# Low parts of four weight tiles and of two batches' probabilities, made by an adding DMA onto the negative of the high parts

## The chip, the core and the metric

The kernel runs on one core of a Trainium2 chip. The metric is device time in microseconds for one execution, from launch to end. The core has a matrix engine (TensorE; PE in the profile, PEld for its weight loads), a vector engine (VectorE, DVE), an activation engine (ScalarE, ACT), a general engine (GpSimd, POOL) and SyncE (SP), which here only issues DMAs. Each engine runs its own instructions in order; they wait for each other through semaphores.

## The reference

Attention through a packed set of 32 queries per head, followed by a feed-forward network with an ELU between its two matrices. For 8 batches, 8 heads, 576 positions and head size 64:

```python
p_packed = sm_attn(p, k, v)          # 32 packed queries read the keys and values
out = sm_attn(q, p_packed, p_packed) # every position reads the 32 packed ones
x = out.transpose(0, 2, 1, 3).reshape(B * S, H * D)      # 4608 x 512
h = x @ w_in                                             # 512 -> 2048
g = np.where(h > 0.0, h, np.exp(np.minimum(h, 0.0)) - 1.0)
return (g @ w_out).astype(np.float32)                    # 2048 -> 512
```

The two weight matrices arrive as 64-bit floating-point words; the core turns them into 32-bit ones itself, from their mantissa, exponent and sign.

## The kernel before

**The products.** The feed-forward input isn't formed. For each batch and each quarter `c` of the 2048 hidden columns, `mstep` multiplies the packed attention result by `w_in` (L705) into a tile `m`; the hidden values are then the probabilities `a` of the second attention times `m` (`mm`, L815 and L822). The hidden columns are taken in 16 tiles of 128, `f` = 0 to 15, and each batch in two halves of its 576 positions. One step of the main loop is one (batch, half, `f`): product `mm`, then ACT's Relu (L829) and Exp (L835), then DVE's maximum (L838), which gives the ELU value `g`, then the second product with `w_out` (`out_mm`, L932 to L941), which is issued 3.5 steps later in the plan.

**High and low parts.** Most products are made in a faster 32-bit format of the matrix engine (`F32R`). An operand is split into a high part, a copy into that format, and a low part, word minus high part; three products of parts stand for one product. For `w_out` the parts are `wo(f, 0)` and `wo(f, 1)`, made by `high` (a copy, on ACT) and `low` (a subtraction, on DVE, L331). For the probabilities they are `a_hi` and `a_lo`, made in `attention` by `hi` (a copy, L252) and `lo` (a subtraction, L658), one pair of instructions per half of a batch. The start works without these parts: batches 0 and 1 use whole words for `c` = 0 (`H_PLAIN`, L815) and for the first four tiles of `w_out` (`F_PLAIN`, L932), whose words lie in `w_words`. Their parts are made all the same, since batches 0 and 1 need `a_hi` and `a_lo` from `f` = 4 on, and batches 2 to 7 need all of `w_out` in parts.

**The weights.** `weights(f, first, prio)` converts one tile of `w_in` (`first`) or of `w_out`: `load` by SP into `raw` (three buffers for both matrices), `exponent` (L280), `sign` (L292), `power` (L287), `mantissa` into `mi` (two buffers, L295), `whole` (L301), the last reader of `raw`, `signed` (L308) and `product` (L318). The product of a `w_in` tile goes to `w_in_sb`, that of the first four `w_out` tiles to `w_words`, that of the others back into `mi`, from which `high` and `low` then read. Tiles `f` of 8 and more lie in `wo_b`, whose memory is that of the first batches' temporary tiles; `home_op` stands for the moment at which these are free.

**The order.** Nothing is put in order by hand. Every operation is entered by `op(prio, engines, function, deps, take, use)` with a due number and an estimated time for each engine that may do it. `schedule()` plays this out greedily: at each moment the ready operation of the lowest due number starts on its engine if the engine and all its buffers are free. Due numbers are steps of the main loop: `first_use` of what is made, less a lead such as `LI`, `LO` or `LM`, or plus `T_WS` (high and low parts of the first four `w_out` tiles) or `T_AS` (those of the first two batches' probabilities). A released buffer is one whose users' estimated ends are past. What the plan gives to each engine is then that engine's order on the chip.

**Output.** Finished sums go through `part` to HBM, first parts by SP, later parts by an adding DMA issued on POOL (L964).

Of the kernel before, what the change touches and what calls it, by code (L numbers as in the profile page):

```python
# [9 lines left out]
F32 = mybir.dt.float32  # L10
# [5 lines left out]
ALU = mybir.AluOpType  # L16
# [4 lines left out]
def packed_attention_elu_ffn(  # L21
# [19 lines left out]
    nc = tc.nc  # L41
# [22 lines left out]
    WC = NPAIR * P  # L64
# [13 lines left out]
    T_ATT, T_ATT1 = [12, 14.0, 15.0, 16.0, 17.5, 17.5], [-12, -11, -11, -10, -10, -9]  # L78
    LI, LO, LM, LOOK = 4.5, 3.0, 2.5, 3.5
    TM = [24.5, 24.5, 28.0, 28.0]  # L80
    T_S2, STAY, SWITCH = 0, 4, 0.12

    F_PLAIN, H_PLAIN = 4, [0, 1]
    T_WS, T_AS = 20, 6

# [55 lines left out]
    def op(prio, on, fn, deps=(), take=(), use=(), after=(), mode=None):  # L145
        o = Op()
        o.prio, o.on, o.fn, o.deps = prio, on, fn, [d for d in deps if d is not None]
        o.after = [d for d in after if d is not None]
        o.take, o.end, o.n, o.mode = list(take), None, len(ops), mode
        for b in list(take) + list(use):  # L150
            b.users.append(o)
        ops.append(o)
        return o

    def schedule():
# [81 lines left out]
        raw=3, ex=2, sg=1, mi=2, p=2, ppT=3, pp=1, k0=1, q0=1,  # L237
# [7 lines left out]
    def wo(f, part):  # L245
        return wo_a[:, f, part, :] if f < NFA else pools["wo_b"][:, f - NFA, part, :]
# [4 lines left out]
    def copy(e, out, in_):  # L251
# [3 lines left out]
    w_ready, w_split, conv_ops = {}, {}, []  # L255

    w_words = [
        Buf(R["m_lo"], lambda: mpool.tile([P, 2, E], F32, tag="m_lo", name="w_words"))
        for _ in range(F_PLAIN // 2)
    ]  # L260

    def weights(f, first, prio):

        raw = ring_tile("raw", stg, [P, WC, 2], U32, "raw", bufs=3)
        ex_b = ring_tile("ex", stg, [P, WC], U16, "ex")
        sg_b = ring_tile("sg", stg, [P, WC], BF16, "sg", bufs=1)
        mi_b = ring_tile("mi", stg, [P, WC], U32, "mi")

        def words():
            r = raw.t  # L270
            top = r.rearrange("p n t -> p (n t)").bitcast(U16).rearrange("p (n t) -> p n t", t=4)
            return r[:, :, 0], r[:, :, 1], top[:, :, 3]

        def load(e):
            nc.sync.dma_start(  # L275
                out=raw.t.rearrange("p n t -> p (n t)"), in_=(w_in if first else w_out)[f]
            )

        def exponent(e):
            nc.vector.tensor_scalar(  # L280
                out=ex_b.t, in0=words()[2], scalar1=4, scalar2=0x7FF,
                op0=ALU.logical_shift_right, op1=ALU.bitwise_and,
            )

        def power(e):

            nc.scalar.activation(  # L287
                out=ex_b.t.bitcast(BF16), in_=ex_b.t, func=AF.Exp, scale=LN2, bias=ebias
            )

        def sign(e):
            nc.scalar.activation(out=sg_b.t, in_=words()[1].bitcast(F32), func=AF.Sign)  # L292

        def mantissa(e):
            nc.vector.tensor_scalar(  # L295
                out=mi_b.t, in0=words()[1], scalar1=0xFFFFF, scalar2=0x100000,
                op0=ALU.bitwise_and, op1=ALU.bitwise_or,
            )

        def whole(e):  # L300
            nc.vector.scalar_tensor_tensor(  # L301
                out=mi_b.t.bitcast(F32), in0=words()[0], scalar=2.0 ** -32, in1=mi_b.t,
                op0=ALU.mult, op1=ALU.add,
            )

        def signed(e):
            pw = ex_b.t.bitcast(BF16)
            nc.vector.tensor_tensor(out=pw, in0=pw, in1=sg_b.t, op=ALU.mult)  # L308

        def product(e):  # L310
            ms, pw = mi_b.t.bitcast(F32), ex_b.t.bitcast(BF16)
            out = ms
            if plain:
                out = word()
            if first:
                out = w_in_sb[:, :, f * P:(f + 1) * P]
                ms, pw = (x.rearrange("p (c f) -> p c f", c=NPAIR) for x in (ms, pw))
            nc.vector.scalar_tensor_tensor(  # L318
                out=out, in0=ms, scalar=2.0 ** -20, in1=pw, op0=ALU.mult, op1=ALU.mult
            )  # L320

        plain = not first and f < F_PLAIN

        def word():
            return w_words[f // 2].t[:, f % 2, :] if plain else mi_b.t.bitcast(F32)

        def high(e):
            copy(e, wo(f, 0), word())

        def low(e):  # L330
            nc.vector.tensor_tensor(  # L331
                out=wo(f, 1), in0=word(), in1=wo(f, 0).bitcast(F32), op=ALU.subtract
            )

        ld = op(-60 + f if first and f < 4 else -44 + f / 9 if f < 2 else prio - 8, {"DMA": 1.45}, load, take=[raw])
        x = op(prio, {"DVE": 0.42}, exponent, [ld], take=[ex_b], use=[raw])
        s = op(prio, {"ACT": 0.66}, sign, [ld], take=[sg_b], use=[raw])
        p = op(prio, {"ACT": 0.72}, power, [x], use=[ex_b])
        m = op(prio, {"DVE": 0.42}, mantissa, [ld], take=[mi_b], use=[raw])
        w = op(prio, {"DVE": 0.69}, whole, [m], use=[raw, mi_b])  # L340
        g = op(prio, {"DVE": 0.42}, signed, [p, s], use=[ex_b, sg_b])
        words_b = w_words[f // 2:f // 2 + 1] if plain else []
        take = words_b if f % 2 == 0 else []
        last = op(
            prio, {"DVE": 0.69}, product, [w, g], take=take,
            use=[mi_b, ex_b] + [b for b in words_b if b not in take],
            after=[w_ready[False, f - 1]] if words_b and f % 2 else [],
        )
        if plain:

            h = op(T_WS + f, {"ACT": 0.61}, high, [last], use=words_b)
            w_split[f] = op(T_WS + f, {"DVE": 0.69}, low, [h], use=words_b)
        elif not first:
            home = [home_op] if f >= NFA else []
            h = op(prio, {"ACT": 0.61}, high, [last] + home, use=[mi_b])
            last = op(prio, {"DVE": 0.69}, low, [h], use=[mi_b])
        w_ready[first, f] = last
        conv_ops.append(last)

# [9 lines left out]
    def attention(b, ts):  # L369

        st, prev_b = Batch(), sts.get(b - 1)
# [18 lines left out]
        whole = b in H_PLAIN  # L390
# [65 lines left out]
        for name, fn, bufs, t in (  # L456
            ("k", load_k, k_b, ts[0] - 6), ("v", load_v, v_b, ts[0] - 5), ("q", load_q, q_b, ts[0] - 3),
        ):
            lds[name] = []
            for n, x in enumerate(bufs):  # L460
                prev_ld = op(
                    t, {"DMA": 3.3 / len(bufs)}, lambda e, fn=fn, n=n: fn(e, n),
                    take=[x] + ([p_b] if (name, n) == ("k", 0) else []), after=[prev_ld],
                )
                lds[name].append(prev_ld)
# [40 lines left out]
        def srec1(e):  # L506
# [6 lines left out]
        o1 = op(ts[0], {"PE": 1.0}, s1, ld_k, take=ps1 + e1s, use=[p_b] + k_b,  # L513
                after=[prev_b.tmp_last if b > 1 else None], mode=1)
        o4s, o = [], None
        for g in range(G):
            o = op(ts[0], {"DVE": 0.76}, lambda e, g=g: smax1(e, g), [o1], use=[ps1[g]], after=[o])
            o = op(ts[0], {"DVE": 0.16}, lambda e, g=g: neg(e, g), [o])
# [4 lines left out]
        for g in range(G):  # L523
# [19 lines left out]
            t = ts[1]  # L543
# [20 lines left out]
        o = op(ts[2], {"PE": 0.85}, pv, ld_v + tr_done, take=[ps, pp_b], use=v_b + e1T, mode=2)  # L564
        done = []
        for g in range(G):
            def norm(e, g=g, ps=ps):
# [10 lines left out]
                use=[ps, pp_b],  # L578
# [11 lines left out]
        o = op(ts[3], {"PE": 0.06}, tr2, done, take=[pt2, st.ppT], use=[pp_b])  # L590
# [3 lines left out]
        for half in range(2):  # L594
            ps = banks(2)
            t1, t2 = temp(), st.af if whole else temp()
# [47 lines left out]
            cs = slice(half * HS, (half + 1) * HS)  # L644

            def done(t2=t2, cs=cs):
                if whole:
                    return st.af.t[:, :G, cs]
                return flat(t2).rearrange("p (g s) -> p g s", g=G)
# [4 lines left out]
            def hi(e, cs=cs, done=done):  # L654
                copy(e, st.a.t[0][:, :, cs], done())

            def lo(e, cs=cs, done=done):
                nc.vector.tensor_tensor(  # L658
                    out=st.a.t[1][:, :, cs], in0=done(), in1=st.a.t[0][:, :, cs].bitcast(F32),
                    op=ALU.subtract,  # L660
                )

            t = ts[4 + half]
            o = op(t, {"PE": 0.52}, s2, [lds["q"][half % len(q_b)], st.ppT_op],
                   take=[ps, t1], use=[q_b[half % len(q_b)], st.ppT], mode=1)
            f0 = op(t, {"DVE": 0.44}, lambda e, fold=fold: fold(e, 0), [o] + prev, use=[ps, t1])
            f1 = op(t, {"DVE": 0.44}, lambda e, fold=fold: fold(e, 1), [f0], use=[ps, t1])
            o = op(t, {"DVE": 0.75}, smax, [f1], use=[t1])
            o = op(t, {"DVE": 0.76}, ssub, [o], use=[t1])
# [11 lines left out]
                t, {"ACT": 0.67, "DVE": 0.4}, hi, [o] + st.a_done[-1:],  # L681
                take=[st.a] if half == 0 else [], use=[t2] + ([st.a] if half else []),
            )
            st.a_done.append(op(t, {"DVE": 0.75}, lo, [h], use=[t2, st.a]))
        st.tmp_last = prev[0]
        st.m, st.m_done = {}, {}
        return st
# [327 lines left out]
```

## Time and profile before

| what | value |
|---|---|
| median of three runs | 725.33 us (725.0 to 726.03) |
| the profiled execution's own time | 724.5 us |
| its span, first to last instruction | 722.3 us |
| granted clock of TensorE, mean | 0.998 |
| PE busy | 699.6 us, 97% of the span |
| PEld busy | 557.1 us, 77% |
| DVE busy | 504.4 us, 70% |
| ACT busy | 387.4 us, 54% |
| POOL busy | 19.4 us, 3% |

The span is the time between the first and the last instruction that the profiler recorded; 2.2 us of the execution's time lie around it. Busy time is the union of an engine's instructions. The shares are means over the whole span: the first hundred microseconds, in which the weights are converted and the first batches run, look different from the rest, so windows of the span are read beside the page. A row of a group shows the line, the engine, the operation, what is written and what is read, and how often; then times. A row of the chain of waits shows the start, the length and what ran.

### The profile page before, as it was taken

Reading aid. Unit: us, or ns where it says so; the run is one execution under the profiler, and the core shown is the slowest. Engines: PE = TensorE matmul, PEld = TensorE weight load, DVE = VectorE, ACT = ScalarE, POOL = GpSimd, SP = SyncE. Lnnn points to the kernel's source line nnn. Section 1 sums busy time; section 2 is a strip of 40 time slices with the busy share of each in tenths; the row PEclk is TensorE's granted clock in tenths of the full one; section 3 lists DMA queues with packets and bytes.
Section 4 is the critical chain, followed back from the end, with each engine's and each line's share of the span. In section 5 each row is a group of like instructions: output and inputs, shape, how many; then the busy total and the mean of one; then the engine's idle time right before and its main releaser. Section 6 shows DMA issues by size and latency. Waiting matters only on the chain.

```text
span 722.3 us, 13401 instructions
## 1 busy us (share of the span) xinstructions
PE 699.6 (97%) x5076; PEld 557.1 (77%) x5076; DVE 504.4 (70%) x1256; ACT 387.4 (54%) x900; POOL 19.4 (3%) x27
## 2 busy tenths in 40 slices
PE   2799999999999999999999999999999999999997
PEld 1454588887778877888878887888888877888886
DVE  6999998886875587545875569555686559654453
ACT  5777888885654455434454445434454345444332
POOL 0000002110111000000000000000000000000000
PEclk9999999999999999999999999999999999999999
DMA  9846546634543430003300250001400040000010
GB/s 348 296 150 204 186 147 142 132 66 108 165 59 44 123 108 1 30 1 128 117 2 29 67 165 1 2 29 66 160 21 1 30 132 30 1 30 1 0 45 30
DMA packets 29360, 61.42 MB, mean 85 GB/s; under 512 B 2544, under 2 KB 11760, under 8 KB 29040
## 3 DMA queue, kind: packets, MB, share of 16 engines
q1 hardware_dynamic: 26272, 55.06, 22.6%
q0 software_dynamic: 3024, 5.51, 5.6%
q8 instruction: 40, 0.66, 0.4%
q14 instruction: 24, 0.20, 0.1%
HBM read 45.61 MB, written 14.94 MB: 84 GB/s over the span
## 4 chain that ended last, share of the span: by engine, by line
PE 96%; DVE 1%; DMA 1%; ACT 1%; issue 0%; SPq 0%; ACTq 0%
PE psum L822 27%; PE psum L938 18%; PE psum L939 17%; PE psum L941 17%; PE psum L932 4%; PE psum L705 4%; PE psum L815 2%; PE psum L557 2%; PE psum L531 1%; PE psum L476 1%; PE psum L602 1%; DMA k<-in_kT 1%; DVE mx L486 0%; ACT tmp L500 0%; SPq L275 0%
## 5 line engine op out<-in xcount | busy, mean ns | idle before, releaser
L829 ACT ACTIVATE e<-psum 128x256 f32<-128x256 f32 (+1 forms) x256 | 105.4, 412 | 236.2 <-PE psum L822 214.4
L838 DVE SCALAR_TENSOR_TENSOR e<-e,psum 128x256 f32<-128x256 f32 (+1 forms) x240 | 103.6, 432 | 106.8 <-ACT e L835 106.1
L822 PE MATMUL psum<-a_hi,m_hi 128*128 128x256 f32 (+1 forms) x480 | 146.5, 305 | 0.0
L822 PE MATMUL psum<-a_lo,m_hi 128*128 128x256 f32 (+1 forms) x480 | 142.0, 296 | 0.0
L822 PE MATMUL psum<-a_hi,m_lo 128*128 128x256 f32 (+1 forms) x480 | 141.9, 296 | 0.0
L861 DVE TENSOR_TENSOR g_lo<-e,g_hi 128x256 fp32r<-128x256 f32 (+1 forms) x240 | 105.3, 439 | 22.0 <-ACT g_hi L252 7.1
L835 ACT ACTIVATE e<-e 128x256 f32<-128x256 f32 (+1 forms) x256 | 114.0, 445 | 6.1
L938 PE MATMUL psum<-wo_b,g_hi 128*128 128x512 f32 x288 | 114.8, 398 | 0.0
L939 PE MATMUL psum<-wo_b,g_hi 128*128 128x512 f32 x288 | 113.6, 394 | 0.0
L822 PEld LDWEIGHTS psum<-a_hi,m_hi 128*128 128x128 f32 x480 | 90.5, 189 | 24.2 <-issue 9.6
L938 PE MATMUL psum<-wo_a,g_hi 128*128 128x512 f32 x252 | 99.4, 394 | 0.0
L939 PE MATMUL psum<-wo_a,g_hi 128*128 128x512 f32 x252 | 99.3, 394 | 0.0
L822 PEld LDWEIGHTS psum<-a_lo,m_hi 128*128 128x128 f32 x480 | 90.7, 189 | 8.7 <-issue 1.0
L822 PEld LDWEIGHTS psum<-a_hi,m_lo 128*128 128x128 f32 x480 | 90.6, 189 | 0.0
L941 PE MATMUL psum<-wo_b,g_lo 128*128 128x512 f32 x288 | 86.6, 391 | 0.0
L941 PE MATMUL psum<-wo_a,g_lo 128*128 128x512 f32 x252 | 76.1, 392 | 0.0
L938 PEld LDWEIGHTS psum<-wo_b,g_hi 128*128 128x128 f32 x288 | 54.2, 188 | 12.1 <-issue 3.6
L941 PEld LDWEIGHTS psum<-wo_b,g_lo 128*128 128x128 f32 x288 | 54.1, 188 | 12.1
L252 DVE CAST g_hi<-e 128x256 fp32r<-128x256 f32 (+1 forms) x180 | 54.0, 300 | 12.5 <-PE psum L939 3.7
L939 PEld LDWEIGHTS psum<-wo_b,g_hi 128*128 128x128 f32 x288 | 54.3, 189 | 7.6
L941 PEld LDWEIGHTS psum<-wo_a,g_lo 128*128 128x128 f32 x252 | 47.3, 188 | 10.5
L938 PEld LDWEIGHTS psum<-wo_a,g_hi 128*128 128x128 f32 x252 | 47.5, 188 | 9.4 <-ACT g_hi L252 2.5
(88 smaller groups left out, 761.3 us busy)
## 6 DMA issues: line engine op xcount, KB each, us to landing
out<-part SPq DMA_DIRECT2D x36, 256.0 KB, 2.2
raw<-in_w_in SPq DMA_DIRECT2D x16, 512.0 KB, 3.7
kvq<-in_v SPq DMA_DIRECT2D x16, 512.0 KB, 5.1
raw<-in_w_out SPq DMA_DIRECT2D x16, 512.0 KB, 3.5
kvq<-in_kT SPq DMA_DIRECT2D x14, 576.0 KB, 4.5
kvq<-in_qT SPq DMA_DIRECT2D x14, 576.0 KB, 4.6
out<-part POOLq DMA_DIRECT2D x21, 256.0 KB, 4.4
k<-in_kT SPq DMA_DIRECT2D x1, 1152.0 KB, 7.4
```

Source lines behind the costliest of these rows:

```text
L252: (nc.scalar.copy if e == "ACT" else nc.vector.tensor_copy)(out=out, in_=in_)
L557: nc.tensor.matmul(ps.t[cols_of(pair), g, :D], lhsT=e1T[g].t[:n, c, cols_of(pair)], rhs=values(c, h)[:n], start=(c == 0), stop=(c == NKC - 1),
L705: nc.tensor.matmul(ps.t[cols_of(pair), g, :w], lhsT=st.ppT.t[rows_of(g), pair, :], rhs=w_in_sb[rows_of(g), pair, c * FC + part * w:c * FC ...
L822: nc.tensor.matmul(ps_b.t[:, :n_tok], lhsT=m_b[x].t[:, g, o:o + P], rhs=st.a.t[y][:, g, cols], start=(n == 0), stop=(n == 3 * G - 1),)
L829: nc.scalar.activation(out=e_b.t[:, :n_tok], in_=ps_b.t[:, :n_tok], func=AF.Relu, scale=-1.0)
L835: nc.scalar.activation(out=x, in_=x, func=AF.Exp, scale=-1.0)
L838: nc.vector.scalar_tensor_tensor(out=out, in0=e_b.t[:, cs], scalar=-1.0, in1=ps_b.t[:, cs], op0=ALU.add, op1=ALU.max)
L861: nc.vector.tensor_tensor(out=g_b.t[1][:, cs], in0=x, in1=g_b.t[0][:, cs].bitcast(F32), op=ALU.subtract)
L932: nc.tensor.matmul(a.t, lhsT=g_b.t[0][:, t].bitcast(F32), rhs=w_words[f // 2].t[:, f % 2, :], start=first, stop=final,)
L938: nc.tensor.matmul(a.t, lhsT=g_b.t[0][:, t], rhs=wo(f, 0), start=first, stop=False)
L939: nc.tensor.matmul(a.t, lhsT=g_b.t[0][:, t], rhs=wo(f, 1), start=False, stop=False)
L941: nc.tensor.matmul(a.t, lhsT=g_b.t[1][:, t], rhs=wo(f, 0), start=False, stop=final)
```

## The change

Two kinds of low parts are no longer made by DVE's subtraction. ACT writes the negative of the word, rounded to the same format, to the place of the low part; a DMA issued on POOL then adds the word itself onto it. That is done for the first four `w_out` tiles (`BY_DMA`) and for the probabilities of batches 0 and 1 (`A_DMA` with `whole`). The due numbers of these parts become smaller (`T_WS` from 20 to 16, `T_AS` from 6 to 2). The word of a later `w_out` tile goes into the first half of `raw` instead of `mi`, and `high` and `low` read it there. The due numbers of the first loads are taken from a list, `FIRST`.

```diff
+    FIRST = "i0 i1 i2 i3 k v o0 o1 q".split()
+    BY_DMA, A_DMA = (0, 1, 2, 3), True
...
-    T_WS, T_AS = 20, 6
+    T_WS, T_AS = 16, 2
...
-            out = ms
-            if plain:
-                out = word()
+            out = word()
...
         def word():
-            return w_words[f // 2].t[:, f % 2, :] if plain else mi_b.t.bitcast(F32)
+            return w_words[f // 2].t[:, f % 2, :] if plain else raw.t[:, :WC // 2].rearrange(
+                "p n t -> p (n t)"
+            ).bitcast(F32)
...
+        def minus(e):
+            nc.scalar.mul(wo(f, 1), word(), -1.0)
+
         def low(e):
-            nc.vector.tensor_tensor(
-                out=wo(f, 1), in0=word(), in1=wo(f, 0).bitcast(F32), op=ALU.subtract
-            )
-
-        ld = op(-60 + f if first and f < 4 else -44 + f / 9 if f < 2 else prio - 8, {"DMA": 1.45}, load, take=[raw])
+            if e == "DVE":
+                nc.vector.tensor_tensor(
+                    out=wo(f, 1), in0=word(), in1=wo(f, 0).bitcast(F32), op=ALU.subtract
+                )
+            else:
+                nc.gpsimd.dma_start(out=wo(f, 1).bitcast(F32), in_=word(), accum_op=ALU.add)
+
+        name = ("i" if first else "o") + str(f)
+        t = FIRST.index(name) - 60 if name in FIRST else prio - 8
+        ld = op(t, {"DMA": 1.45}, load, take=[raw])
...
             prio, {"DVE": 0.69}, product, [w, g], take=take,
-            use=[mi_b, ex_b] + [b for b in words_b if b not in take],
+            use=[mi_b, ex_b] + [b for b in words_b if b not in take] + [raw] * (not (first or plain)),
...
             h = op(T_WS + f, {"ACT": 0.61}, high, [last], use=words_b)
-            w_split[f] = op(T_WS + f, {"DVE": 0.69}, low, [h], use=words_b)
+            if f in BY_DMA:
+                h = op(T_WS + f, {"ACT": 0.61}, minus, [h], use=words_b)
+            w_split[f] = op(T_WS + f, {"POOL": 1.0} if f in BY_DMA else {"DVE": 0.69}, low, [h], use=words_b)
         elif not first:
             home = [home_op] if f >= NFA else []
-            h = op(prio, {"ACT": 0.61}, high, [last] + home, use=[mi_b])
-            last = op(prio, {"DVE": 0.69}, low, [h], use=[mi_b])
+            h = op(prio, {"ACT": 0.61}, high, [last] + home, use=[raw])
...
+            last = op(prio, {"POOL": 1.0} if f in BY_DMA else {"DVE": 0.69}, low, [h], use=[raw])
...
+            if b == 0:
+                t = FIRST.index(name) - 60
...
+            def minus(e, cs=cs, done=done):
+                nc.scalar.mul(st.a.t[1][:, :, cs], done(), -1.0)
+
+            def add(e, cs=cs, done=done):
+                nc.gpsimd.dma_start(
+                    out=st.a.t[1][:, :, cs].bitcast(F32), in_=done(), accum_op=ALU.add
+                )
...
-            st.a_done.append(op(t, {"DVE": 0.75}, lo, [h], use=[t2, st.a]))
+            if whole and A_DMA:
+                h = op(t, {"ACT": 0.67}, minus, [h], use=[t2, st.a])
+                h = op(t, {"POOL": 1.0}, add, [h], use=[t2, st.a])
+            else:
+                h = op(t, {"DVE": 0.75}, lo, [h], use=[t2, st.a])
+            st.a_done.append(h)
```

More of the change, by code (lines that the diff above doesn't have):

```diff
@@ L351, in weights @@
             h = op(T_WS + f, {"ACT": 0.61}, high, [last], use=words_b)
-            w_split[f] = op(T_WS + f, {"DVE": 0.69}, low, [h], use=words_b)
+            if f in BY_DMA:
+                h = op(T_WS + f, {"ACT": 0.61}, minus, [h], use=words_b)
+            w_split[f] = op(T_WS + f, {"POOL": 1.0} if f in BY_DMA else {"DVE": 0.69}, low, [h], use=words_b)
         elif not first:
             home = [home_op] if f >= NFA else []
-            h = op(prio, {"ACT": 0.61}, high, [last] + home, use=[mi_b])
-            last = op(prio, {"DVE": 0.69}, low, [h], use=[mi_b])
+            h = op(prio, {"ACT": 0.61}, high, [last] + home, use=[raw])
+            if f in BY_DMA:
+                h = op(prio, {"ACT": 0.61}, minus, [h], use=[raw])
+            last = op(prio, {"POOL": 1.0} if f in BY_DMA else {"DVE": 0.69}, low, [h], use=[raw])
         w_ready[first, f] = last
```

## The prediction

> **What bounds the kernel now.** I read the page's 40 slices first, then the waits of PE, the chain of waits in order of time, and the windows. The waits of PE, longest first (what waited, for what: us in total, times, longest us):
>
> ```profile
> PE psum L476 <- DMA k<-in_kT: 10.1, 1, 10.1
> PE psum L531 <- ACT tmp L500: 5.9, 3, 2.8
> PE psum L476 <- ACT m_hi L252: 1.1, 1, 1.1
> ...
> PE psum L815 <- DVE g_hi L838: 0.2, 1, 0.2
> ```
>
> All but the last of these lie before the first L815 matmul, at 31.6 us. After that PE waits 0.2 us in all. The page warns that a busy PE need not be a PE at its peak, so the chain of waits has to be asked whether matmuls follow each other at one pace (start us, us, what):
>
> ```profile
> 68.14 0.86 PE psum L815 x4
> 69.00 2.58 PE psum L932 x6
> 71.58 0.86 PE psum L815 x4
> ```
>
> Every piece begins where the one before it ends: four L815 matmuls of 256 columns at 0.215 us each, six L932 of 512 columns at 0.43 us each, and so on. There is no idle time hidden in the busy time here. DVE, which the change relieves, is the fullest of the other engines in these stretches (PE, PEld, DVE, ACT, POOL busy us; PE clock; DMA share; GB/s):
>
> ```profile
> 20.00:30.00 10.00, 5.53 (x114) 2.41 (x103) 9.20 (x21) 6.86 (x15) 0.00 (x0) 1.00 0.96 347
> 30.00:40.00 10.00, 9.35 (x109) 6.76 (x108) 9.00 (x22) 8.05 (x21) 0.00 (x0) 0.83 0.64 203
> 60.00:70.00 10.00, 9.85 (x46) 5.41 (x45) 9.89 (x23) 9.48 (x22) 0.00 (x0) 1.00 0.59 189
> 100.00:120.00 20.00, 20.00 (x120) 16.87 (x119) 17.01 (x43) 16.31 (x41) 1.92 (x2) 1.00 0.56 158
> ```
>
> So there are two stages. Before 31.6 us a chain through ACT and DVE sets the time, with PE idle about half. Afterwards PE sets it, and DVE, though 9.9 of 10 us busy at 60 to 70 us, delivers just in time: nearly nobody waits for it. A microsecond taken from DVE after 31.6 us is worth at most the 0.2 us that PE waits; a microsecond taken before it is worth something only on the chain.
>
> **The change part by part.** These are the instructions removed, and the nearest relatives of those added (ns min/median/max, first and last start):
>
> ```profile
> L331 DVE TENSOR_TENSOR wo_a<-w_words,wo_a x4: 674/684/685, 26.0 to 80.1; 128x512 fp32r<-128x512 f32 x4
> L658 DVE TENSOR_TENSOR a_lo<-k,a_hi x2: 694/723/752, 38.3 to 41.5; 128x576 fp32r<-128x576 f32 x2
> L658 DVE TENSOR_TENSOR a_lo<-q,a_hi x2: 747/751/755, 61.8 to 68.2; 128x576 fp32r<-128x576 f32 x2
> L252 ACT CAST wo_a<-w_words x4: 620/633/639, 21.2 to 39.1; 128x512 fp32r<-128x512 f32 x4
> L252 ACT CAST a_hi<-k x2: 657/666/674, 31.1 to 40.8; 128x576 fp32r<-128x576 f32 x2
> 109.94 1.92 POOL L964 DMA_DIRECT2D out<-part  x2 [108.64 <-ACT part L252]
> out<-part POOLq DMA_DIRECT2D x21, 256.0 KB, 4.4
> ```
>
> DVE loses 4 x 0.684 + 2 x 0.723 + 2 x 0.751 = 5.7 us. ACT gains as many scaled copies: 4 x 0.633 + 4 x 0.666 = 5.2 us, with the price of the cast of the same tile. POOL gains eight issues of about 0.96 us (1.92 us for two stores), and it stands idle until 108.6 us, so nothing is queued behind them at first. Seven to eight microseconds of work move, but only the part that touches a bound counts.
>
> *Start, DVE.* One removed subtraction falls before 31.6 us. The rows of batch 0's softmax around it (start us, us, engine, line, operation):
>
> ```profile
> 25.73 0.69 ACT L626 ACTIVATE tmp<-tmp 128x576 f32<-128x576 f32 x1 [0.56 <-DVE tmp L620]
> 25.96 0.67 DVE L331 TENSOR_TENSOR wo_a<-w_words,wo_a 128x512 fp32r<-128x512 f32 x1
> 26.56 0.73 DVE L630 TENSOR_REDUCE sm<-tmp 128x18 f32<-128x576 f32 x1
> 27.23 0.74 DVE L486 TENSOR_REDUCE mx<-psum 128x1 f32<-128x576 f32 x1
> 30.27 0.77 DVE L652 STREAM_TRANSPOSE k<-tmp 128x576 f32<-128x576 f32 x1
> 31.64 2.37 PEld L815 LDWEIGHTS psum<-k,m_hi 128*128 128x128 f32 x7
> ```
>
> The subtraction runs while the exponential (to 26.42 us) holds the chain anyway; the sum L630 comes 0.14 us later. Taking it away gives 0.14 us at least, at most its own 0.67 us if DVE's following fill also moves forward. I take -0.1, since the row right behind it says so. The next of the subtractions on weights stands far behind:
>
> ```profile
> 62.88 0.68 DVE L331 TENSOR_TENSOR wo_a<-w_words,wo_a 128x512 fp32r<-128x512 f32 x1
> ```
>
> So the other seven removed operations start after 31.6 us and are worth between 0 and the 0.2 us that PE waits there; I take 0. DVE's saved time will be filled by weight conversion that has later due times.
>
> *Start, ACT.* A negative copy follows each high part. ACT's idle places there:
>
> ```profile
> 22.38 0.62 ACT L252 CAST wo_a<-w_words 128x512 fp32r<-128x512 f32 x1 [0.54 <-DVE w_words L318]
> 27.71 0.65 ACT L292 ACTIVATE sg<-raw 128x512 bf16<-128x512 f32 x1 [1.30 <-DMA raw<-in_w_out]
> ```
>
> The first copy of 0.63 us fits into a hole of 0.54 and pushes the next cast by 0.1; the second goes into the hole of 0.56 before L626 or the one of 1.30 us. Cost: 0 to 0.6 us; I take +0.1.
>
> *After the start, ACT.* Six more copies fall on an engine that is up to 9.48 of 10 us busy, and each is not interrupted once begun. Where ACT is fullest, the chain already leaves PE:
>
> ```profile
> 62.77 0.24 ACT wo_a L252
> ...
> 63.68 0.50 DVE g_hi L838
> 64.22 1.34 PE psum L815 x4
> ```
>
> An ELU chain (Relu, Exp, DVE maximum) that meets a copy just begun is up to 0.67 us late; two products in flight and the next batch's matmuls cover it nearly everywhere. Bounds: 0 (all hidden) and 6 x 0.65 = 3.9 us; I take +0.2, the size of the one wait of this kind that the rows show.
>
> *The adds.* Their nearest row is the store by adding DMA, 4.4 us to landing. Their results are late only beyond this (ns and first and last start):
>
> ```profile
> L822 PE MATMUL psum<-a_lo,m_hi x480: 278/294/311, 81.8 to 712.1; 128*128 128x256 f32 x80, 128*128 128x320 f32 x80
> L932 PE MATMUL psum<-w_words,g_hi x72: 590/592/697, 37.3 to 88.5; 128*128 128x512 f32 x72
> ```
>
> The first reader of a low probability starts at 81.8 us, while the last of the subtractions replaced is at 68.2; the four weight tiles' low parts aren't read before batch 2, as batches 0 and 1 multiply by the whole words, until 88.5 us. Over 12 us of slack stand against 0.96 + 4.4 = 5.4 us for issue and landing: 0, and a loss only from more than twice that landing time on. The Trainium skill, "SBUF — State Buffer", section "SBUF: two separate sides", speaks against adds issued here: GpSimd can't write their descriptors while a DVE instruction in a two-port mode holds the shared port. No row of before isolates this; the 0.96 us per issue while DVE is 85% busy bears out no long lock. In traffic, one add of 256 KB at the 347 GB/s of 20 to 30 us takes 0.75 us; two beside the first loads delay those by 0 to 1.5 us. They bring batch 1's keys and values, off batch 0's chain: 0.
>
> *The raw buffer.* From the fifth w_out tile on, the word is kept in raw instead of mi, so raw (three buffers, shared with w_in) stays taken until the low part is made. Loads wait for just that release now:
>
> ```profile
> SPq L275 <- DVE mi L301: 80.6, 22, 8.2
> raw<-in_w_in SPq DMA_DIRECT2D x16, 512.0 KB, 3.7
> 102.99 6.38 SPq L275 DMA_DIRECT2D raw<-in_w_in  x2
> 118.91 0.68 DVE L331 TENSOR_TENSOR wo_b<-mi,wo_b 128x512 fp32r<-128x512 f32 x1
> 120.18 0.42 DVE L280 TENSOR_SCALAR ex<-raw 128x512 uint16<-128x512 uint16 x1
> 131.93 0.69 DVE L318 SCALAR_TENSOR_TENSOR w_in_sb<-mi,ex 128x512 f32<-128x512 f32 x1
> 134.24 0.66 PE L705 MATMUL psum<-w_in_sb,ppT 64*32 64x256 f32 x16
> ```
>
> The tightest place: the second of those loads goes out at about 109.0, after L301 of the eleventh w_out tile. With the new release it goes out after that tile's L331, at 119.6, and lands 3.7 us later, at 123.3; its first reader stands at 120.2, so 3.1 us late. Its conversion now takes until 132.6 with pauses of some microseconds in between, and PE needs it at 134.2, 1.6 us of slack. Cost 0 if the pauses shrink, 3.1 - 1.6 = 1.5 us if they don't. In return mi is free earlier, and DVE comes to this stage with up to 5.7 us less behind it: I take 0. A load that waits at the head of SP's queue also holds back the keys, queries and plain stores behind it; these are planned with the same releases, so it is the same term.
>
> The due times of the high and low parts (20 to 16, 6 to 2) move idle-time work; the new list of first loads gives the old order (four of w_in, k, v, two of w_out, q), and is worth 0.
>
> **Sum** against the profiled execution: 724.5 us, 722.3 of span and 2.2 around it. -0.1 + 0.1 + 0.2 + 0 = +0.2, so 724.7. The median of the runs shown, 725.33, is 0.8 above that execution; the forecast on that scale is 725.5.
>
> **Rivals.**
> *Faster: the start shortens.* The chain to 31.6 us carries DVE work not of its own, L486 at 27.23 for one; if the new plan drops one such block, 0.7 us go. One stretch of the start is also clocked down (same columns as the windows above):
>
> ```profile
> 30.20:33.60 3.40, 2.87 (x10) 2.48 (x11) 3.37 (x10) 3.06 (x8) 0.00 (x0) 0.50 0.59 215
> ```
>
> From 31.6 to 33.6 PE runs the bound work at half speed, so 1.0 us is lost there; a plan that keeps PE busier before it would win that, and 0.7 + 1.0 = 1.7 gives 723.6. Against it: the matmuls before it hang on the same waits as now. The Trainium skill, "TensorE: Matmul & The Clock Gate", Part 1, says that an idle window of about 3.4 us halves the clock and that the windows run free of the kernel. The row agrees: 3.4 us at 0.50, behind a stretch in which PE was busy 5.5 of 10 us. By that rule a small shift of the window could also cost as much again, which would give 726.5.
>
> *Slower: the raw buffer starves conversion.* Price 1.5 us at the place above, and once more for the last tiles of w_in, which pass the same three buffers: 725.5 + 3.0 = 728.5. It decides when low parts of w_out wait more than 1.6 us longer than PE's next weights allow. For it: all 22 of the waits above. Against it: mi freed earlier, and DVE time.
>
> *Slower: ACT takes DVE's place.* If three of the six copies land on an ELU chain, 3 x 0.65 = 2.0 us: 727.5. For it, ACT's 9.48 of 10; against it, PE's contiguous pieces.
>
> *Late adds.* From the end of the last replaced subtraction, 68.9, to the first reader, 81.8, there are 12.9 us; issue and landing take 5.4. An add that took 16 us would cost the 3.1 us beyond: 728.6.
>
> *The change doesn't do what it says*: DVE's time is refilled by other work in the same stretch, and PE never learns of it: 725.3.
>
> **Chances.** Forecast (723.9 to 726.8) 0.56; refilled, 0.05; shorter start 0.19; raw buffer 0.10; ACT 0.08; late adds 0.02. A measurement of this kernel can tell about 0.2%, 1.45 us, from no change. So faster 0.19, same 0.61, slower 0.20. The range reaches from 723.2 (just beyond the short start) to 728.0, leaving the tails of the slow cases outside.
>
> **What would show it.** In the changed profile the first L815 should still start within 0.7 us of 31.6, and PE's waits behind it should stay under 1 us. L331 should have 12 rows and L658 12, ACT about 5 us more between 20 and 75 us. Loads of raw should wait for L331 in place of L301. The forecast is wrong if PE waits for L705's weights near 105 to 165 us, or for g_hi between 34 and 80 us, or if the first L815 starts below 30 us.

## The result, and the profile after

The changed kernel takes 729.78 us (median of 4 runs, 728.37 to 730.66) against 725.16 us of the kernel before (four runs, the three of the table above among them): a ratio of 1.0059, 95% interval 1.0044 to 1.0074. It is slower by 0.6%, where no change was forecast, with 728.0 us as the upper end of the range. The profiled execution took 730.66 us, 6.2 us more than the one before; the difference of the medians is 4.6 us. Of the 6.6 us by which its span is longer (728.9 against 722.3), 2.8 us are idle time of PE (25.5 against 22.7) and 3.8 us busy time (703.4 against 699.6, with 5076 matmuls both times). The granted clock differs from run to run, 0.992 to 0.994 in the four runs of the change and 0.992 to 1.000 in 26 of the kernel before, so this split holds for one execution.

The waits of PE in the changed kernel (what waited, for what: us in total, times, longest us; L845 is what L815 was, L574 was L557, L600 was L583):

```profile
PE psum L493 <- DMA k<-in_kT: 10.1, 1, 10.1
PE psum L548 <- ACT tmp L517: 5.7, 2, 2.9
PE psum L574 <- DMA kvq<-in_v: 2.8, 2, 2.1
PE psum L600 <- ACT pp L586: 1.2, 2, 0.7
PE psum L493 <- DMA kvq<-in_kT: 0.6, 1, 0.6
...
PE psum L845 <- DVE ri L525: 0.3, 1, 0.3
```

New is the third row: the matmuls on batch 1's values wait for a load. The same windows as before (PE, PEld, DVE, ACT, POOL busy us; PE clock; DMA share; GB/s), and PE's two stretches at half clock:

```profile
20.00:30.00 10.00, 5.99 (x107) 2.47 (x97) 8.68 (x20) 8.69 (x17) 2.13 (x3) 1.00 0.94 277
30.00:40.00 10.00, 6.65 (x86) 4.90 (x87) 6.11 (x14) 4.56 (x13) 0.65 (x1) 0.75 0.91 278
31.60:35.00 3.40, 3.13 (x9) 2.43 (x8) 3.37 (x9) 2.04 (x6) 0.00 (x0) 0.50 1.08 300
38.40:45.20 6.80, 5.51 (x58) 4.39 (x59) 3.48 (x10) 3.48 (x9) 1.20 (x1) 0.50 0.48 149
60.00:70.00 10.00, 10.00 (x56) 4.54 (x55) 9.09 (x22) 7.35 (x16) 1.38 (x2) 1.00 0.85 247
100.00:120.00 20.00, 20.00 (x119) 17.05 (x118) 16.76 (x45) 16.47 (x41) 1.81 (x2) 1.00 0.52 147
```

The loss sits in 30 to 45 us. From 30 to 40 PE is 6.65 us busy, where it was 9.35; DVE and ACT fall too; the likely reason is that the products which they read aren't made yet. The DMA engines, at 0.64 of their time before, are 0.91 full. From 38.4 to 45.2 us PE runs at half clock, twice as long as in the one stretch that the kernel before has (30.2 to 33.6 us) and that the changed kernel has as well, a little later (31.6 to 35.0). At full clock its 5.51 us of work there would take about half as long: 2.8 us lost, an estimate from this row. From 60 us on the rows are those of a PE that waits for nobody, as before. The chain of waits through the hole (start us, us, what):

```profile
20.68 5.46 DMA kvq<-in_kT
...
27.44 0.64 SPq L457
...
28.18 10.73 DMA kvq<-in_v
38.92 0.04 issue
38.96 1.50 PE psum L574 x40
```

One load of values takes 10.73 us and sets the end of the stage. The first landings of values, from the rows of their issuing line in the stretch from 20 us, first in the kernel before, then in the changed one (ns of the issue, first and last start; us from issue to landing):

```profile
L438 SPq DMA_DIRECT2D kvq<-in_v x2: 379/472/566, 26.5 to 27.5; - x2
...
DMA to landing us min/median/max: 6.1/6.3/6.5
```

```profile
L453 SPq DMA_DIRECT2D kvq<-in_v x2: 378/472/567, 27.0 to 28.2; - x2
...
DMA to landing us min/median/max: 10.4/10.6/10.7
```

The loads go out 0.5 to 0.7 us later and land 4.9 us later (28.2 + 10.7 = 38.9 against 27.5 + 6.5 = 34.0). Three adds onto weight tiles were under way at that time: issued at 22.8, 26.7 and 29.8 us, they landed 9.7, 8.3 and 7.9 us later, at 32.5, 35.0 and 37.7. Their rows, and the DMA queues before and after (packets, MB, share of 16 engines' time over the span):

```profile
22.83 1.05 POOL L342 DMA_DIRECT2D wo_a<-w_words  x1 [21.52 <-ACT wo_a L334]
26.73 0.86 POOL L342 DMA_DIRECT2D wo_a<-w_words  x1 [2.85 <-ACT wo_a L334]
29.79 0.86 POOL L342 DMA_DIRECT2D wo_a<-w_words  x1 [2.20 <-DVE sm L650]
```

```profile
q1 hardware_dynamic: 26272, 55.06, 22.6%
q0 software_dynamic: 3024, 5.51, 5.6%
```

```profile
q1 hardware_dynamic: 26272, 55.06, 22.1%
q0 software_dynamic: 4688, 7.74, 7.5%
```

Queue q0 carries POOL's transfers. Before, these were 21 adding stores: 5.6% of 722.3 us is 40.4 us, 1.9 us of all 16 engines for each 256 KB. SP's transfers on q1, loads and plain stores, need 22.6% of 722.3 = 163 us for 55.06 MB, 0.78 us for the same 256 KB (0.262 MB). So by this share an adding transfer is dear, and a row of before said so. The eight adds of the change take 7.5% of 728.9 less 40.4 = 14 us, 1.8 us each. These shares are rough. They add up the times of packets, which can overlap (in the changed kernel the share is 1.08 from 31.6 to 35.0 us), and the same 21 stores read 5.4 to 5.9% in the seven runs of this study that have no other transfer on q0. Of the lock that the prediction names nothing is seen: the adds were issued in 0.86 to 1.05 us while DVE was 87% busy.

### The profile page after: what moved, and what is told of

It is laid out like the page before. It is cut to its first block, busy times and chain, and to the rows that moved or that the text cites. A ratio compares the mean times of both kernels' runs of the same rounds, so it can differ in the third digit from the quotient of the medians.

```text
span 728.9 us, 13431 instructions
## 1 busy us (share of the span) xinstructions
PE 703.4 (97%) x5076; PEld 560.0 (77%) x5076; DVE 500.7 (69%) x1249; ACT 391.4 (54%) x907; POOL 27.6 (4%) x35
## 3 DMA queue, kind: packets, MB, share of 16 engines
q1 hardware_dynamic: 26272, 55.06, 22.1%
## 4 chain that ended last, share of the span: by engine, by line
PE 95%; DMA 3%; SPq 0%; ACT 0%; DVE 0%; issue 0%
PE psum L852 27%; PE psum L968 18%; PE psum L969 17%; PE psum L971 17%; PE psum L962 4%; PE psum L735 4%; PE psum L845 2%; PE psum L574 2%; DMA kvq<-in_v 1%; PE psum L493 1%; PE psum L548 1%; PE psum L619 1%; DMA k<-in_kT 1%; DMA kvq<-in_kT 1%; SPq L278 0%
```

## The experiments

Three theories were set against the first. A: the adds' transfers fill DMA engines that are full anyway, and loads that PE needs become late. B: ACT's additional copies make the start or ELU chains late. C: the raw buffer, held longer, starves conversion. D: the planner's new order is worse by itself. Where a kernel keeps the changed kernel's order of instructions, it tells A and B apart without D. All ratios are to the kernel before on the same chip.

### Four kernels of one order: adds and copies of the weight tiles

`e1_no_weight_adds` leaves the adds out, `e10_adds_no_copies` the copies, `e12_neither` both.

```diff
# e1
-                nc.gpsimd.dma_start(out=wo(f, 1).bitcast(F32), in_=word(), accum_op=ALU.add)
+                pass
# e10: the copy left out, the add onto the high part, the high part read for the low
-            nc.scalar.mul(wo(f, 1), word(), -1.0)
+            pass
-                nc.gpsimd.dma_start(out=wo(f, 1).bitcast(F32), in_=word(), accum_op=ALU.add)
+                nc.gpsimd.dma_start(out=wo(f, 0).bitcast(F32), in_=word(), accum_op=ALU.add)
     def wo(f, part):
+        part = 0 if f in BY_DMA else part
# e12: both left out, part as in e10
```

> The changed kernel with the four adds onto w_out's low parts left out, so that these low parts stay the negative of the high parts; every other instruction and its order is that of the changed kernel. Theory A (the three adds issued before 31 us fill DMA engines that are full already, so batch 1's values land at 39.1 us instead of 34.2, and PE waits for them): the last of the values lands by 35 us, PE waits for values under 0.5 us, time 724.5 to 726.5. Theory B (ACT's additional copies make the start late) and theory C (the raw buffer, held longer, makes conversion late) and theory D (the new order itself is worse): these are all still in, so 729 to 730.7.

> The changed kernel without ACT's negative copies for the four w_out tiles; the adds stay in place and go onto the high parts, which then also stand for the low parts in the products. The order is that of the changed kernel. Theory A (the adds' transfers cost): values land at 38 us or later, 728.5 to 730.5. Theory B (the copies cost): 726 to 727.

> The changed kernel without the negative copies and without the adds for the four w_out tiles; the high parts stand for the low parts in the products; order as in the changed kernel. Without the adds alone 726.65 us were measured; what this is below it is the price of the four copies on ACT. If copies at the start cost nothing: 726 to 727. If they are the rest of the loss: 725 to 725.8.

| | without the adds | with the adds |
|---|---|---|
| without the copies | e12: 725.94 us, 1.0012 (0.9992 to 1.0033) | e10: 730.43 us, 1.0062 (1.0045 to 1.0080) |
| with the copies | e1: 726.65 us, 1.0019 (1.0005 to 1.0033) | the change: 729.78 us, 1.0059 (1.0044 to 1.0074) |

The adds are worth 0.40% with the copies (1.0059 - 1.0019) and 0.50% without (1.0062 - 1.0012), 2.9 and 3.6 us; the intervals of each pair lie apart. The copies are worth +0.07% and -0.03%, nothing that can be told; e12 came out between its two expectations. In e1 the values land as before (the same rows as above, then PE's waits):

```profile
L453 SPq DMA_DIRECT2D kvq<-in_v x2: 378/452/527, 26.7 to 27.7; - x2
...
DMA to landing us min/median/max: 5.5/5.8/6.1
```

```profile
PE psum L600 <- ACT pp L586: 1.3, 2, 0.8
PE psum L619 <- DMA kvq<-in_qT: 0.8, 1, 0.8
```

The wait for values is gone. The DMA engines have room again (windows of e1, columns as above):

```profile
20.00:30.00 10.00, 6.25 (x107) 2.82 (x100) 8.68 (x21) 8.90 (x19) 0.00 (x0) 1.00 0.92 332
30.00:40.00 10.00, 8.67 (x109) 6.38 (x108) 8.37 (x20) 7.39 (x20) 1.35 (x1) 0.83 0.60 189
```

From 20 to 30 us they are as busy as with the adds (0.92 against 0.94) but move 332 GB/s where they moved 277; from 30 to 40 us they are 0.60 busy in place of 0.91, as the loads are done sooner. This is the same order of instructions, so the adds alone make the loads late. In e10 the adds hurt another load first (PE's waits):

```profile
PE psum L494 <- DMA k<-in_kT: 10.3, 1, 10.3
PE psum L549 <- ACT tmp L518: 5.3, 2, 2.8
PE psum L494 <- DMA kvq<-in_kT: 4.1, 1, 4.1
...
PE psum L575 <- DMA kvq<-in_v: 0.9, 2, 0.7
```

Here PE waited 4.1 us for batch 1's keys and 0.9 us more for the values, so the time expected by theory A came, but by another load than expected: which of the loads in flight pays isn't fixed.

### What an add costs against a copy

`e2_plain_copies` keeps everything but makes the four adds plain copies.

```diff
-                nc.gpsimd.dma_start(out=wo(f, 1).bitcast(F32), in_=word(), accum_op=ALU.add)
+                nc.gpsimd.dma_start(out=wo(f, 1).bitcast(F32), in_=word())
```

> The changed kernel with the four adds onto w_out's low parts replaced by plain copies of the same 256 KB from the same queue, so that the low parts become the words; the order is the same. Theory A1 (an add takes the DMA engines about 1.7 us against some 0.7 us of a plain transfer of that size, as it also reads its destination): values land at about 36 to 37 us, time 726 to 728. Theory A2 (any transfer of that size does it, or GpSimd's issue): values at about 39 us, time 729 to 730.7. Theories B, C, D: 729 to 730.7.

727.39 us, 1.0040 (1.0022 to 1.0058): in A1's range, but the interval overlaps that of the change and that of e1, so the time doesn't decide between A1 and A2. The queue of POOL's transfers without the four adds (e1), then with copies in their place (e2):

```profile
q0 software_dynamic: 4112, 6.69, 6.7%
```

```profile
q0 software_dynamic: 4432, 7.74, 6.9%
```

Four copies take 0.2% of 727.4, 1.5 us, or 0.4 us each; four adds take 7.5% of 728.9 less 6.7% of 724.7, 6.1 us, or 1.5 us each. As the share of the same 21 stores differs by up to half a per cent between runs, each of these may be off by some 0.6 us. Beside the loads the first three copies landed after 8.3, 6.5 and 6.1 us, the adds after 9.7, 8.3 and 7.9; the fourth, in a quieter place, landed after 3.4 us as a copy and 3.3 us as an add. All this points to a dearer add, but its price isn't settled. Nor are copies shown to be harmless: PE's idle time in e2's profile is that of the change (727.4 - 701.9 and 728.9 - 703.4 are both 25.5 us), with 3.1 us of waiting for batch 1's keys and none for the values.

### The adds on probabilities

`e5_no_adds` also leaves those out, in the same order.

```diff
-                nc.gpsimd.dma_start(
-                    out=st.a.t[1][:, :, cs].bitcast(F32), in_=done(), accum_op=ALU.add
-                )
+                pass
```

> The changed kernel with all eight adds left out, so that the low parts of the first four w_out tiles and of two batches' probabilities stay the negative of the high parts; order unchanged. Without the four on weights alone 726.65 us were measured. If the adds on probabilities also cost something, as they run beside batch 1's queries: 725 to 726. If not (what is left, 1.4 us over before, then comes of ACT's copies and of the order): 726.3 to 727.

726.06 us, 1.0007 (0.9992 to 1.0021). That is 0.12% or 0.9 us below e1, within the intervals: a cost of these four adds is not shown. Nor does anything remain that could be told from the kernel before: without adds, the change's order and copies cost 0.07%.

### The raw buffer and the due times

`e6_raw_only` is the changed kernel without adds and copies and with the old due times; `e8_words_in_mi` is the change with the words back in `mi`; `e7_due_only` is the kernel before with the new due times.

```diff
# e6
-    BY_DMA, A_DMA = (0, 1, 2, 3), True
+    BY_DMA, A_DMA = (), False
-    T_WS, T_AS = 16, 2
+    T_WS, T_AS = 20, 6
# e7, of the kernel before
-    T_WS, T_AS = 20, 6
+    T_WS, T_AS = 16, 2
# e8
-            return w_words[f // 2].t[:, f % 2, :] if plain else raw.t[:, :WC // 2].rearrange(
...
+            return w_words[f // 2].t[:, f % 2, :] if plain else mi_b.t.bitcast(F32)
```

> Of the change only the word in raw instead of mi, and the list of first loads; no adds and no negative copies, due times 20 and 6 as before. Theory C (the raw buffer, held longer, starves conversion): 728 to 730, with waits of PE for weights or for the ELU chain between 100 and 170 us. Otherwise 724.5 to 726.

> The changed kernel with the words of the later w_out tiles in mi again, so that raw is released as before; adds, copies and due times stay. Theory A: 728.5 to 731, values late as in the changed kernel. If the raw buffer is a good part of the loss: 726 to 728.

> The kernel before with the due times 16 and 2 in place of 20 and 6, nothing else. If the earlier due times load DVE and ACT while ELU chains are short of time: 726.5 to 729, with waits of PE for the ELU chain between 45 and 115 us. Otherwise 724.5 to 726.

e6 took 725.06 us, 1.0002 (0.9989 to 1.0015): theory C falls. e8 took 732.16 us, 1.0097 (1.0077 to 1.0117), more than the change and more than theory A expected. Its order is another one, so it can't be read from this that the raw buffer helps; nor is there a sign in it that the loss is raw's. e7 took 726.48 us, 1.0018 (1.0003 to 1.0033), just at the lower end of what an effect would give; but its profile has no wait of PE for an ELU chain, and the expected place isn't confirmed. If the earlier due times cost 0.18%, these runs don't show where.

### Other plans for the same work

In `e3_adds_wait` the copies and adds of the weight tiles wait for batch 1's packed result. `e4_probs_only` has no adds on weights at all. `e9_old_due` is the change with the old due times. In `e11_all_wait` all eight copies wait for the end of batch 1's second softmax, with the old due times. The planner made a new order for each.

```diff
# e3
-                h = op(T_WS + f, {"ACT": 0.61}, minus, [h], use=words_b)
+                h = op(T_WS + f, {"ACT": 0.61}, minus, [h, sts[1].ppT_op], use=words_b)
# e4
-    BY_DMA, A_DMA = (0, 1, 2, 3), True
+    BY_DMA, A_DMA = (), True
# e11, besides T_WS, T_AS = 20, 6
-                h = op(T_WS + f, {"ACT": 0.61}, minus, [h], use=words_b)
+                h = op(T_WS + f, {"ACT": 0.61}, minus, [h, sts[1].af_done[1]], use=words_b)
...
+    for h in sts[0].copies + sts[1].copies:
+        h.deps.append(sts[1].af_done[1])
```

> The changed kernel with one dependency more: the negative copies and adds of the four w_out tiles wait for batch 1's packed result, so that these adds come after batch 1's values have been used. The planner makes its order anew. Theory A: values land by 35 us, the adds move to 37 us and later, where they collide with nothing that PE waits for; time 723.5 to 726.5. Theory B: part of ACT's load also moves away from the start, at most the 0.3 us by which the first L845 matmul starts later now, so 729 to 730. Theories C and D: 728 to 731.

> The changed kernel with w_out's low parts by DVE's subtraction again; the probabilities' adds, the raw buffer and the due times stay. Theory A: no add before 37 us, values by 35 us, time 724 to 726.5. Theory C: the raw buffer is still held longer, 728 to 731. Theory B: half of ACT's copies remain, about 727 to 728.

> The changed kernel with the due times of before, 20 and 6. The first adds are issued when ACT and POOL are idle and so as early as now. Theory A: values late, 728.5 to 731. If the due times are what makes the change slow: 725 to 727.

> The changed kernel with the due times of before, and with all eight negative copies (and so the adds) waiting for the end of batch 1's second softmax, near 58 us, when no load that PE is near to needing is under way. Theory A: the start is as in the kernel before, values by 35 us, time 724.3 to 725.8, so no gain over before either, as PE has no waits that DVE causes. If DVE's relief were worth something on PE's side: below 724. If the copies on ACT meet ELU chains after 58 us: 726 to 728.

| | time | ratio |
|---|---|---|
| e3 | 728.01 us | 1.0032 (1.0017 to 1.0047) |
| e4 | 729.86 us | 1.0069 (1.0043 to 1.0094) |
| e9 | 731.44 us | 1.0067 (1.0045 to 1.0089) |
| e11 | 732.42 us | 1.0091 (1.0059 to 1.0124) |

Only e9 came as theory A had it, a little above its range: due times do not hold back work on an idle engine. e3 is 1.5 us above what A expected, e4 and e11 are 3.4 and 6.6 us above, though in these two batch 1's values landed early enough for PE not to wait for them. In e4, PE waits at 63 us, and there theory B's mechanism can be seen (chain of waits):

```profile
61.59 0.44 ACT e L859
62.03 0.57 ACT a_lo L675
62.60 0.36 ACT e L865
62.97 0.02 issue
62.99 0.50 DVE g_hi L868
63.49 0.04 issue
63.53 1.34 PE psum L845 x4
```

The negative copy `a_lo` stands between Relu and Exp of the product that PE needs next, for 0.57 us, and PE waited 1.0 us there, of which the copy can be charged with 0.57 at most. In e11 the chain from 79 us ran over a store of 5.53 us and a load of raw behind it. So the question was asked once more with e11's order held fixed: `e13_wait_no_adds` leaves its adds out, `e14_wait_neither` also its copies, with the same edits as in e5 and e12 (for `a_lo` the high part is read).

> The kernel in which all copies and adds wait for batch 1's second softmax, with all eight adds left out (the low parts stay the negative of the high parts); order unchanged. That kernel took 732.42 us although its start was on time; its chain of waits at 79 to 93 us runs over a store of 5.5 us, the copy into part that waited for it, and a load of raw behind them in SP's queue. Theory A (the adds' transfers make the transfers of others late wherever they run): 725 to 727, store and load near 2 and 3.5 us again. Theory B (ACT's copies meet the ELU chains): 730 to 732.5. Theory D (the order): 730 to 732.5.

> The same kernel without adds and without negative copies; the high parts stand for the low parts of the first four w_out tiles and of two batches' probabilities. What it is below the run without adds alone is the price of eight copies on ACT at this place: 0 to 0.5 us if they are covered (theory A), 2 to 5 us by theory B.

e13 took 731.15 us, 1.0072 (1.0047 to 1.0098); e14 730.79 us, 1.0064 (1.0040 to 1.0087). Theory A, stretched to e11, falls: most of its loss stays when adds and copies are gone. So does theory B for this order, as e14 is only 0.4 us below e13 where 2 to 5 were expected. What stays is put down to the order, theory D, as the only theory left. The chain of waits in e14 shows one place:

```profile
110.73 0.40 DVE g_lo L893
111.13 0.35 DVE mi L299
...
111.51 0.69 DVE mi L305
112.20 0.40 DVE g_lo L893
112.60 0.60 DVE wo_b L339
113.20 0.41 DVE e L870
113.61 0.04 issue
113.65 0.50 PE psum L970
```

Mantissa, `whole` and a low part of `w_out`, 1.6 us together, stand on DVE ahead of the maximum L870 that PE waits for. PE's waits in e14 have the price, and in the profiled run more is lost by the clock (last section):

```profile
PE psum L620 <- DMA kvq<-in_qT: 2.5, 2, 2.0
PE psum L970 <- DVE e L870: 1.9, 1, 1.9
```

### What DVE's relief is worth

`e15_before_no_lows` is the kernel before, in its own order, without the eight subtractions and with nothing in their place.

```diff
-            nc.vector.tensor_tensor(
-                out=wo(f, 1), in0=word(), in1=wo(f, 0).bitcast(F32), op=ALU.subtract
-            )
+            if not plain:
+                nc.vector.tensor_tensor(
+                    out=wo(f, 1), in0=word(), in1=wo(f, 0).bitcast(F32), op=ALU.subtract
+                )
# the subtraction of the probabilities likewise under "if not whole:"
     def wo(f, part):
+        part = 0 if f < F_PLAIN else part
```

> The kernel before with the eight subtractions that the change replaces left out, and nothing in their place (high parts stand for low parts in those products); the order is that of before. It is the most that relief of DVE can bring. If PE sets the time after 31 us, as the prediction has it: 724.5 to 725.6, no gain beyond 0.3 us. If DVE's 5.7 us are worth something on PE's side: 720 to 723.5.

It took 725.64 us, where the kernel before took 726.54 in the same runs; the ratio of the runs is 0.9996 (0.9977 to 1.0014), so the two can't be told apart; the interval reaches to a gain of 0.23%. The window of before that was fullest now reads

```profile
60.00:70.00 10.00, 9.85 (x46) 5.36 (x45) 8.70 (x20) 9.56 (x23) 0.00 (x0) 1.00 0.55 180
```

DVE fell from 9.89 to 8.70 us busy, and PE has the same 9.85.

## Why the prediction was wrong, point by point

**What bounds the kernel: right.** PE sets the time after 31.6 us, and DVE's relief alone is worth 0.04%, not distinguishable from nothing (e15; the interval reaches to 0.23%). But that PE sets the time there also means that any operand which comes later than PE's turn costs time, and the values were such an operand.

**The start, DVE and ACT: right within its terms.** The first L845 starts at 32.03 us where it started at 31.64; +0.0 was forecast for the sum of the two terms and 0.7 was named as the bound. The copies on ACT cost nothing measurable in the change itself (e1 against e12, the change against e10). As a mechanism, the ACT rival exists: in e4 a copy stands in the chain that PE waits for.

**The raw buffer: right.** A cost of 0 was taken; e6 measured 1.0002.

**The adds: wrong, and this is the step that failed.** The prediction priced one at 0.75 us from the GB/s of the loads, bounded two at 1.5 us together, and took 0, because the loads beside them bring "batch 1's keys and values, off batch 0's chain". The price is probably too low: the nearest row was q0's share, 1.9 us of all engines for each adding store of the same size, and the four weight adds came out at about 1.5 us each by the same rough measure. Three of them were issued before 31 us, not two, since the planner starts a ready copy whenever ACT is idle. The cover failed for certain: the values of batch 1 landed at 34.0 us before, and PE's matmul on them began at 34.56. That is 0.6 us of slack. PE works in order, so work off batch 0's chain is still in its way. In the changed kernel they landed 4.9 us later, and without the four adds, in the same order, PE didn't wait for them (e1). Three adds of 1.5 us and the later issue (0.5 to 0.7) would be 5.0 to 5.2 us; that this is so near to 4.9 is partly luck, as the 1.5 is rough and the later issue may itself come from the first add.

**The rivals.** "Late adds" asked when the adds' own readers would suffer, and their slack of 12.9 us was real: in the changed kernel the last add onto `a_lo` was issued at 69.8 us, none took over 7.0 us to land, and the first reader came at 88.4. What it didn't ask is who shares the DMA engines. The slower rivals that were given, raw buffer and ACT, are not the cause. The clock was priced at 1.0 us on either side; it worked on the slower one. In the two stretches at half clock of the changed profile PE was busy 3.13 and 5.51 us, in the one of before 2.87, so by estimate the clock took (8.64 - 2.87) / 2 = 2.9 us more, as much as the 2.8 us of added idle time.

**The sum.** Of +0.59%, 0.40 to 0.50% are the adds on weights. The four on probabilities (0.12%) and the rest (0.07%) can't be told from nothing.

**The signs that were named.** The start came as said, and the subtractions that are left have 12 rows each. PE's waits behind the start didn't stay under 1 us, which is the failure above. ACT was busy 39.7 us from 20 to 75 us, where it was 41.3, and not 5 us more. Loads of `raw` waited for `low` (L338) 5 times and still for `whole` (L304) 13 times.

**Smaller slips.** The slack of over 12 us holds for the probabilities; for the weight tiles the last subtraction ended at 80.8 us and the first matmul on their parts came at 90.4, which leaves 9.6. POOL's idle time of 108.64 us ended at 109.9, not at 108.6. The 723.6 of the shorter start is counted from 725.3 and the other rivals from 725.5; on their scale it is 723.8. None of this moves the forecast.

**Another place for the adds.** None of the versions that put the adds elsewhere is faster than the kernel before. By e15 there is nothing to win here that could be measured: a free removal of the eight subtractions brings nothing that shows.

## What to carry to other kernels

Before work is moved to a DMA, price it by the share that its own kind of transfer has of the DMA engines, rough as that is, rather than by the rate of plain loads, and look at what is in flight at the place where it will be issued: the landing of each load and the first instruction that reads it. An engine that is full but that nobody waits for has nothing to give; leave work out altogether, in the same order, before an effort is made to move it. And when a planner makes the order anew for every edit, a comparison tells of the edit only if the order is held fixed: in this study a new order without adds and copies still cost 0.6% (e14).

## What the runs showed of the hardware

Loads by SP and adds by POOL share the DMA engines in time: beside three adds the loads of values took 10.6 us to land, without them 5.8 us in the same order (e1). The Trainium skill says as much in "DMA: Bandwidth & Descriptors", section "Issuing engines are not separate DMA queues": transfers issued by different engines run on the same 16 DMA engines and interleave.

A stall of PE can cost twice. After the wait of 1.9 us in e14, the row shows (columns as in the windows above)

```profile
114.40:117.60 3.20, 3.20 (x11) 2.59 (x11) 2.20 (x5) 2.96 (x7) 0.00 (x0) 0.54 0.93 219
```

PE ran at 0.54 of its clock for 3.2 us, so by estimate about 1.5 us more were lost. In the changed kernel the stretch from 38.4 to 45.2 us at 0.50, behind an idle stretch of PE of 2.1 us, did the same: 2.8 us on top of the waits. PE was idle for less than 3.4 us on end in both places, so the idle window of the prediction need not be idle throughout. Nor does every such stall have this price. In e11 PE waited 2.0 us until 117.25 us, and in e13 1.9 us until 114.77; behind both the clock stayed full, here in e11:

```profile
117.30:120.70 3.40, 3.40 (x18) 2.92 (x19) 2.79 (x6) 3.32 (x8) 0.00 (x0) 1.00 1.00 195
```
